# A new hand-written list of steps for the first three token blocks of a fused retention and snake-activation kernel

## The chip, the cores and the metric

The kernel runs on one core of one Trainium2 chip. The metric is device microseconds of one execution of the whole program on that core. The engines are named as in the profile: PE (TensorE, matmuls and transposes), DVE (VectorE), ACT (ScalarE), POOL (GpSimd), SP (SyncE, which here only issues DMAs).

## The reference, cut to what matters

Eight batches of 576 tokens with 8 heads of 64 go through a causal retention with a decay of its own for each head, and the result, with the heads side by side, is the input of a two-layer feed-forward net with a snake activation.

```python
scores = scale * q @ k^T                      # q, k, v: (8, 8, 576, 64) float32
ret    = scores * Dmat                        # Dmat[i, j] = gamma_h ** (i - j) for j <= i, else 0
attn   = ret @ v
x      = attn.transpose(0, 2, 1, 3).reshape(4608, 512)
h      = x @ w_in                             # 512 x 2048
g      = h + sin(alpha * h) ** 2 / (alpha + 1e-9)
out    = g @ w_out                            # 2048 x 512, float32
```

## The kernel before, in words

**Tiling.** The 4608 tokens are nine blocks of 512. Block n (0 to 7) holds the first 512 tokens of batch n; block 8 gathers the last 64 tokens of all batches. A batch's 512 tokens are two halves of 256, called p = 0 and p = 1; q, k and v of one batch and half are one tile of 512 KB in float32. Retention is done in chunks of 128: the scores of a chunk against itself (`scores`, then the mask by `masked` on DVE, L370), those times v (`values`, L400), and the state that the chunks before left (`outer`, L298, makes a chunk's sum of k and v; `take_sum` or `evict` copies it out of PSUM; `more`, L339 and L340, and `to_state`, L332, decay and add on POOL; `add_states`, L422, multiplies by q). `keep` copies the outcome into xT, a block's input.

**A block's feed-forward net.** The 2048 hidden features are 16 units of 128, called fc. `project(n, fc)` is four matmuls of 128x128 by 512 tokens against w_in (L535). Then come `sine` on ACT (L543), `square` on ACT, DVE or POOL (L552, L554) and `product` on DVE (L559), which writes gT. For blocks 0 and 1 `gemm2(n, u, tag)` does the second layer: u = 4c + part, c one of four groups of 128 tokens, part one of four quarters of w_out; each is four matmuls of 512 columns (L581). `finish(n, c)` copies a group out and stores it. From block 2 on the second layer is done by sums and products of halves (`Quarters`, L652), which needs sums of halves of w_out that `weigh(k, i)` makes (L602).

**Loads.** `load(b, nm, p)` issues one 512 KB tile on SP's queue (L121); six of these tiles have buffers (the tag "raw", bufs=6), so a load further on waits until a `cast` has read an older tile. `cast` brings a tile to half precision with the decay factors (L181 for q and k, L104 or L102 for v). The weights come in quarters by `load_w_in(g)` and `load_w_out(g)` on POOL's own DMA queue (L92, L95): 128x4x512 elements, float32 in DRAM and float16 in SBUF. For batches 0 and 1 q and k are transposed on PE (`turn`, L215) and copied out (`take`); from batch 2 on by DMA (`crossed`, L205, on SP).

**What sets the order.** The block `with tc.manual_schedule()` is a hand-written list of calls: every engine and every DMA queue runs its instructions in the order of that list, and an instruction that waits holds up all that stand behind it on its engine. Before the loop, the list covers retention of batches 0 to 4 and the nets of blocks 0, 1 and 2; the loop `for n in range(3, NBLK)` that follows does block n beside the retention of batch n + 1. `keep_busy` puts matmuls of zeros on PE; `told(x, engine)` puts a no-op on an engine that waits for instruction x.

In the list before, q(0,1) and k(0,1) are cast whole on POOL and DVE, w_in's quarters are issued in the order 0, 2, 1, 3, retention of batch 0 is done before the first `project`, block 0's units follow in the order 2, 1, 0, 8, 3, 11, 6, ... with two halves only where a piece is marked 0 or 1, batch 1's retention stands after the last of them among seven `gemm2` calls, and the other nine `gemm2` calls of block 0 stand among block 1's units.

## Time and profile before

| | us |
|---|---|
| median of 3 runs | 302.8 (300.9 to 302.86) |
| the profiled execution, its own time | 300.74 |
| its span | 299.0 |
| PE busy in the span | 284.0 (95%) |
| DVE, ACT, POOL busy | 224.0, 206.3, 196.7 |
| first `project` matmul on PE | 21.35 |
| first `project` of block 1 | 50.58 |
| first `project` of the loop (block 3) | 112.74 |

Times inside the program are microseconds from the start of the span. A row of the timeline gives the start, the length, the engine, the line, the operation with the tile written and the tiles read, the count, and in brackets the idle time of the engine just before it and what ended that wait. SPq, POOLq and ACTq are DMA issues. PEclk in the table of windows is the granted share of PE's full clock.

### The profile page before, as it was taken

The page shows a single profiled execution, that of the slowest core. Times are in us where ns is not written, and L with a number is a line of the kernel's source. Part 1 is how long each engine was busy: PE and PEld are TensorE (multiplying, and loading weights), DVE is VectorE, ACT ScalarE, POOL GpSimd, SP SyncE. Part 2 cuts the span into 40 slices and gives each one's busy share as a digit, 9 for nine tenths or more (in the row PEclk, how much of TensorE's full clock was granted, in tenths as well). Part 3 has the DMA queues.
Part 4 walks back from the last instruction along what each step waited for, and adds up shares of the span by engine and source line. Part 5 has one row for each costly group of instructions (what it writes and reads, how often), then busy time and mean ns, then how long its engine had stood idle before and what let it go on. Part 6 is the DMA issues. An engine that isn't in the chain of part 4 may idle for free.

```text
span 299.0 us, 8721 instructions
## 1 busy us (share of the span) xinstructions
PE 284.0 (95%) x3597; PEld 183.4 (61%) x3597; DVE 224.0 (75%) x316; ACT 206.3 (69%) x328; POOL 196.7 (66%) x186
## 2 busy tenths in 40 slices
PE   7689989999997999999999999999999999999993
PEld 6565545554442576665666666766666666665782
DVE  2597988789779897998779667876778476656871
ACT  1439944876546599776878787878777878887600
POOL 5794680899999789599897789769915900370000
PEclk9689999999999999999999999999999999999998
DMA  7999999999995397978699777587747201310225
GB/s 227 343 217 216 216 251 303 202 299 301 177 248 186 84 166 173 248 179 198 157 271 175 160 184 206 57 190 158 147 108 176 53 3 39 71 37 17 61 49 120
DMA packets 119159, 49.89 MB, mean 167 GB/s; under 512 B 69824, under 2 KB 118096, under 8 KB 119120
## 3 DMA queue, kind: packets, MB, share of 16 engines
q1 hardware_dynamic: 114528, 45.04, 65.8%
q0 software_dynamic: 4224, 4.19, 8.3%
q8 instruction: 28, 0.46, 0.7%
q10 hardware_dynamic: 368, 0.11, 0.2%
q14 instruction: 11, 0.09, 0.1%
HBM read 36.74 MB, written 9.44 MB: 154 GB/s over the span
## 4 chain that ended last, share of the span: by engine, by line
PE 59%; DMA 14%; POOL 11%; DVE 7%; issue 3%; ACT 2%; SPq 2%; POOLq 0%; DVEq 0%; ACTq 0%
PE hps L535 27%; PE hps L652 26%; DMA v<-in_v_dram 10%; DMA q<-in_q_dram 4%; POOL T L602 3%; POOL q L181 2%; DVE ret L370 2%; DVE gT L559 2%; POOL kvs L340 1%; ACT s_t L543 1%; PE o L400 1%; PE ops L581 1%; POOL s L339 1%; PE sc L358 1%; SPq L121 1%
## 5 line engine op out<-in xcount | busy, mean ns | idle before, releaser
L559 DVE SCALAR_TENSOR_TENSOR gT<-ss_t,inva,hps 128x512 f16<-128x512 f16 x144 | 105.6, 744 | 37.8 <-ACT ss_t L552 36.4
L543 ACT ACTIVATE s_t<-hps,alpha_t 128x512 f16<-128x512 f32 x144 | 96.7, 682 | 40.4 <-PE hps L535 39.7
L535 PE MATMUL hps<-xT,w_in 128*128 128x512 f16 (+1 forms) x564 | 121.2, 360 | 2.0 <-DVE gT L559 1.4
L535 PEld LDWEIGHTS <-w_in 128*128 128x128 f16 x628 | 60.1, 98 | 54.7 <-issue 3.3
L552 ACT ACTIVATE ss_t<-s_t 128x512 f16<-128x512 f16 x117 | 73.2, 630 | 3.2
L652 PEld LDWEIGHTS <-gT 128*128 128x128 f16 x656 | 63.9, 98 | 14.4
L624 POOL TENSOR_TENSOR gT<-gT,d 128x1024 f16<-128x1024 f16 x12 | 25.2, 2121 | 29.2 <-PE hps L652 28.1
L652 PE MATMUL hps<-T,gT 128*128 128x256 f16 x336 | 39.8, 273 | 0.0
L652 PE MATMUL hps<-w_out,gT 128*128 128x256 f16 x320 | 38.2, 273 | 0.0
L370 DVE TENSOR_TENSOR ret<-sc,mask 128x1024 f16<-128x1024 f32 (+1 forms) x32 | 34.8, 1117 | 3.8 <-PE sc L358 3.8
L672 DVE TENSOR_TENSOR osb<-osb,hps 128x512 f32<-128x512 f32 x35 | 24.0, 686 | 14.8 <-PE hps L652 13.7
L581 PE MATMUL ops<-w_out,gT 128*128 128x512 f16 x128 | 30.8, 379 | 2.1 <-DVE gT L559 1.4
L181 POOL TENSOR_TENSOR q<-q,cn 128x1024 f16<-128x1024 f32 (+1 forms) x16 | 27.8, 1747 | 4.1 <-DMA q<-in_q_dram 4.1
L630 POOL TENSOR_TENSOR gT<-gT 128x1024 f16<-128x1024 f16 x12 | 25.7, 2161 | 0.0
L181 POOL TENSOR_TENSOR k<-k,cn 128x1024 f16<-128x1024 f32 (+1 forms) x13 | 21.9, 1681 | 1.9 <-DMA k<-in_k_dram 1.9
L581 PEld LDWEIGHTS <-gT 128*128 128x128 f16 x128 | 11.9, 98 | 16.3 <-DVE gT L559 1.9
L340 POOL TENSOR_TENSOR kvs<-s,kvs 128x256 f32<-128x256 f32 x22 | 17.4, 789 | 3.7 <-ACT kvs L102 2.0
L332 POOL TENSOR_TENSOR s<-kvs,cn 128x256 f16<-128x256 f32 x21 | 14.2, 678 | 7.1 <-ACT kvs L102 6.5
L102 ACT COPY osb<-hps 128x512 f32<-128x512 f32 (+2 forms) x15 | 8.2, 549 | 13.5 <-PE hps L652 13.4
L102 ACT CAST xT<-o 128x1024 f16<-128x1024 f32 (+1 forms) x14 | 13.2, 956 | 5.6 <-PE o L422 5.6
L104 POOL CAST v<-v 128x1024 f16<-128x1024 f32 (+1 forms) x10 | 10.0, 1015 | 9.2 <-PE hps L535 6.7
L554 DVE TENSOR_TENSOR ss_t<-s_t 128x512 f16<-128x512 f16 x23 | 12.7, 554 | 3.2 <-ACT s_t L543 3.2
(77 smaller groups left out, 272.8 us busy)
## 6 DMA issues: line engine op xcount, KB each, us to landing
out_dram<-osb SPq DMA_DIRECT2D x70, 128.0 KB, 2.5
q<-in_q_dram SPq DMA_DIRECT2D x16, 512.0 KB, 5.7
k<-in_k_dram SPq DMA_DIRECT2D x10, 512.0 KB, 6.2
v<-in_v_dram SPq DMA_DIRECT2D x10, 512.0 KB, 5.8
k<-in_k_dram SPq DMA_DIRECT2D x24, 128.0 KB, 3.6
v<-in_v_dram SPq DMA_DIRECT2D x24, 128.0 KB, 3.4
w_in<-in_moe_w_in_dram POOLq DMA_DIRECT2D x4, 512.0 KB, 12.0
w_out<-in_moe_w_out_dram POOLq DMA_DIRECT2D x4, 512.0 KB, 11.5
```

Of the source, the lines that this page charges most:

```text
L102: eng.copy(d_, s_)
L181: eng.tensor_tensor(dst[:, a0:a1].rearrange("p a r t d -> p t (a r) d"), t_.rearrange("p (t a) x -> p t a x", t=2)[:, :, a0:a1].rearrange( ...
L370: nc.vector.tensor_tensor(ret.rearrange("p t (z x) -> p (t z) x", z=2)[:, :, 0:n], sc.rearrange("p t (z x) -> p (t z) x", z=2)[:, :, 0:n], ...
L535: matmul(hps_of[n, fc][0][:, cols], w_in16[:, a, fc * P : (fc + 1) * P], xs[n][:, a, cols], start=(a == 0 and part != 1), stop=(a == KT - ...
L543: nc.scalar.activation(s_t, hps, mybir.ActivationFunctionType.Sin, bias=0.0, scale=alpha_t[:, fc : fc + 1],)
L552: nc.scalar.activation(ss_t, s_t, mybir.ActivationFunctionType.Square)
L559: nc.vector.scalar_tensor_tensor(gT[n][:, :, fc, :], ss_t.rearrange("p (t n) -> p t n", t=2), inva[:, fc : fc + 1], hps.rearrange("p (t n) ...
L581: matmul(ops[n, c, cols.start][:, cols], gT[n][:, c // 2, fk, c % 2 * P : c % 2 * P + P], w_out16[:, fk, cols], start=(fk == 0), stop=(fk ...
L624: eng.tensor_tensor(self.part(0, 0, i), self.part(1, 1, i), self.d3[:, 4 * i : 4 * i + 4], SUB)
L630: eng.tensor_tensor(out_, self.part(1, 0, i), self.part(0, 0, i), SUB)
L652: matmul(self.ps[name][:, 256 * m + cols.start : 256 * m + cols.stop], left(j)[:, P * m : P * m + P], right(j)[:, cols], start=(tag is not ...
L672: nc.vector.tensor_tensor(out_, a, self.ps[ps], ADD)
```

## The change

The list of steps up to block 2 is written anew; the functions it calls stay as they are, but that `cast` now returns its instruction and the slots of batch 1's q tiles are swapped.

- Start: all six tiles of batch 0 are loaded first, each cast is done by halves of the heads, and every half is transposed, copied and used as it comes. `load_w_in(0)` and `load_w_in(1)` are put on POOL's queue behind a no-op that waits for the second half of q(0,0)'s cast; quarters 2 and 3 follow later, in the order in which the units need them.
- Block 0: the units go in order 0 to 15. Units 0 to 3 are begun with the first 256 tokens, before `values(1)` of batch 0. Six squares stand on POOL (2, 4, 6, 8, 10, 12) where there were four (3, 7, 12, 10), and between them the half casts of k(1,0) and q(1,0) and the quarters of w_out.
- Batch 1 is worked half by half after block 0's last unit, p = 0 first, among fourteen `gemm2` calls that fill three token groups side by side (banks h0, op and h2) and a fourth (h1); the last two `gemm2` calls of block 0 stand in block 1. `load_w_out(3)` stands behind batch 1's first `to_state`.
- `next_sum(3)` on DVE becomes `more(3)` on POOL, for batches 0 and 1. The two `weigh(1, ..)` now stand ahead of the two casts of batch 2's v.
- Block 1's units go in order 0 to 15; `gemm2(1, 0..2)` moves up into it. In block 2, square 11 and the cast of v(4,1) go from DVE to ACT, `weigh(4, 1)` from DVE to POOL. In the loop at n = 3, three of the six casts are put behind the two `s4` steps on POOL.

```diff
         load(0, "k", 0)
         load(0, "q", 0)
-        cast(0, "q", 0, V, (1,))
+        load(0, "v", 0)
+        load(0, "q", 1)
+        load(0, "k", 1)
+        load(0, "v", 1)
+        cast(0, "k", 0, V, (0,))
         cast(0, "k", 0, V, (1,))
-        cast(0, "k", 0, G_, (0,))
...
+        cast(0, "q", 0, V, (0,))
+        turned = cast(0, "q", 0, V, (1,))
+        told(turned, G_)
+        load_w_in(0)
+        load_w_in(1)
...
+        project(0, 0, "h0", 0)
+        project(0, 1, "h1", 0)
+        project(0, 2, "op", 0)
+        at[0].values(1, False, "m0")
         at[0].values(1, True)
         at[0].add_states(1)
+        at[0].keep(1, A_, V)
...
+        sine(0, 2)
+        square(0, 2, G_)
+        load_w_out(0)
...
+        square(0, 10, G_)
+        load_w_out(2)
+        turn(1, "k", 0, "m1")
+        project(0, 11, "h0")
...
+        at[1].outer((0,), "m0")
+        at[1].evict((0,), A_)
+        at[1].to_state(0, G_)
+        load_w_out(3)
+        at[1].more(1)
...
+        at[1].outer((1,), "m0")
+        at[1].evict((1,), A_)
+        at[1].more(2)
+        at[1].to_state(2, G_)
+        gemm2(0, 7, "h0")
...
+        at[1].more(3)
+        weigh(1, 0, G_)
         cast(2, "k", 1, V, (0,))
         load(3, "k", 1)
+        at[1].to_state(3, G_)
+        weigh(1, 1, G_)
+        cast(2, "v", 1, G_)
         cast(2, "v", 0, G_)
-        weigh(1, 0, G_)
-        weigh(1, 1, G_)
...
-        weigh(4, 1, V)
...
+        square(2, 11, A_)
+        cast(4, "v", 1, A_)
...
-        square(2, 11, V)
-        product(2, 11)
-        cast(4, "v", 1, V)
...
         at[3].to_state(0, G_)
+        weigh(4, 1, G_)
...
+            ahead = 3 if n == 3 else 6
             if n < 6:
-                for x in KEYS:
+                for x in KEYS[:ahead]:
                     cast(n + 2, *x, G_)
             Q.s4(0, G_)
             Q.s4(1, G_)
+            if n < 6:
+                for x in KEYS[ahead:]:
+                    cast(n + 2, *x, G_)
```

The orders below are those of the built programs. A name is a tile with its number: s_t and ss_t are the sine and its square, k32, q32 and v32 loaded tiles, k16, q16 and v16 cast ones, kvs and s32 the sums of a state, s16 and sS states, T1 what `weigh(1, ..)` makes. POOL while block 0's units run, before: the casts of batch 1 are whole ones, and few squares stand between them.

```order
L95 DMA w_out16_72<-in_moe_w_out_dram 128x4x512
L181 TENSOR_TENSOR q16_548<-q32_482,cn_66 128x2x8x64
L554 TENSOR_TENSOR ss_t_589<-s_t_579 128x512
L95 DMA w_out16_72<-in_moe_w_out_dram 128x4x512
L332 TENSOR_TENSOR sS_73<-kvs_229,cn_66 128x256
L95 DMA w_out16_72<-in_moe_w_out_dram 128x4x512
L554 TENSOR_TENSOR ss_t_636<-s_t_634 128x512
L181 TENSOR_TENSOR k16_684<-k32_682,cn_66 128x2x8x64
```

The same place on POOL now, from the square of unit 2 to that of unit 10:

```order
L554 TENSOR_TENSOR ss_t_554<-s_t_552 128x512
L95 DMA w_out16_72<-in_moe_w_out_dram 128x4x512
L554 TENSOR_TENSOR ss_t_575<-s_t_573 128x512
L181 TENSOR_TENSOR k16_586<-k32_294,cn_66 128x2x4x64
L554 TENSOR_TENSOR ss_t_596<-s_t_594 128x512
L95 DMA w_out16_72<-in_moe_w_out_dram 128x4x512
L554 TENSOR_TENSOR ss_t_618<-s_t_616 128x512
L181 TENSOR_TENSOR k16_586<-k32_294,cn_66 128x2x4x64
L554 TENSOR_TENSOR ss_t_639<-s_t_637 128x512
```

The second half of the cast of k(1,0) stands behind four squares, two issues of w_out and its own first half; on PE `turn(1, "k", 0)` waits for it ahead of unit 11.

POOL around the end of batch 1's states, before: the two casts of batch 2's v stand right behind the states, `weigh(1, ..)` follows, and then the casts of q(2,1) and q(3,1).

```order
L340 TENSOR_TENSOR kvs_835<-s32_1007,kvs_835 128x256
L104 CAST v16_1064<-v32_1062 128x1024
L104 CAST v16_1070<-v32_1060 128x1024
L602 TENSOR_TENSOR T1_1072<-w_out16_72 128x512 x2
L602 TENSOR_TENSOR T1_1075<-w_out16_72 128x512 x2
L181 TENSOR_TENSOR q16_1122<-q32_1120,cn_66 128x2x8x64
L181 TENSOR_TENSOR q16_1345<-q32_1124,cn_66 128x2x8x64
```

And now, from the sums that wait for `evict((1,))` on:

```order
L340 TENSOR_TENSOR kvs_827<-s32_1009,kvs_827 128x256
L332 TENSOR_TENSOR s16_829<-kvs_827,cn_66 128x256
L339 TENSOR_TENSOR s32_1088<-kvs_827,cn_66 128x256
L340 TENSOR_TENSOR kvs_827<-s32_1088,kvs_827 128x256
L602 TENSOR_TENSOR T1_1091<-w_out16_72 128x512 x2
L332 TENSOR_TENSOR sS_73<-kvs_827,cn_66 128x256
L602 TENSOR_TENSOR T1_1099<-w_out16_72 128x512 x2
L104 CAST v16_1102<-v32_889 128x1024
L104 CAST v16_1104<-v32_887 128x1024
L181 TENSOR_TENSOR q16_1141<-q32_1139,cn_66 128x2x8x64
L181 TENSOR_TENSOR q16_1352<-q32_1143,cn_66 128x2x8x64
```

`weigh(1, ..)`, one sum and two states moved ahead of the v casts; from the cast of q(2,1) on POOL's list is the same as before up to the last state of batch 3.

SP's queue behind batch 2's first five tiles, before: two transposes, then q(2,1) and q(3,1).

```order
L121 DMA k32_1068<-in_k_dram 128x8x128
L205 DMA_TRANSPOSE kT_1114<-k16_1112 128x8x128
L205 DMA_TRANSPOSE qT_1118<-q16_1116 128x8x128
L121 DMA q32_1120<-in_q_dram 128x8x128
L121 DMA q32_1124<-in_q_dram 128x8x128
```

And now:

```order
L574 DMA out_0_dram<-osb_1038 64x512 x2
L574 DMA out_0_dram<-osb_1079 64x512 x2
L574 DMA out_0_dram<-osb_1084 64x512 x2
L121 DMA k32_1096<-in_k_dram 128x8x128
L205 DMA_TRANSPOSE kT_1133<-k16_1131 128x8x128
L205 DMA_TRANSPOSE qT_1137<-q16_1135 128x8x128
L121 DMA q32_1139<-in_q_dram 128x8x128
L121 DMA q32_1143<-in_q_dram 128x8x128
```

Three stores of block 0's outcome moved ahead of the load of k(3,1), the transposes and the load of q(2,1).

More of the change, by code (lines that the diff above doesn't have):

```diff
@@ L864 @@
[L864 to L883 removed]
+        product(0, 0)
@@ L897 @@
+        square(0, 12, G_)
+        cast(1, "q", 0, G_, (0,))
+        project(0, 13, "op")
+        sine(0, 13)
+        square(0, 13, A_)
+        product(0, 12)
+        product(0, 13)
+        cast(1, "q", 0, G_, (1,))
+        take(1, "k", 0, A_, (0,))
+        take(1, "k", 0, V, (1,))
+        project(0, 14, "m0")
+        sine(0, 14)
+        square(0, 14, V)
+        project(0, 15, "h2")
+        product(0, 14)
+        turn(1, "q", 0, "m1")
         sine(0, 15)
         square(0, 15, A_)
+        gemm2(0, 4, "h0")
@@ L899 @@
+        gemm2(0, 12, "op")
+        take(1, "q", 0, V, (0,))
+        take(1, "q", 0, A_, (1,))
         product(0, 15)
[L900 to L913 removed]
```

457 lines of the change are left out of this document (213 added, 244 removed).

## The prediction, made before the run

> **What bounds the kernel now.** I read the profile's totals and its chain of waits first, then POOL's and PE's timelines, then a table of windows between the points that these gave. Totals, and the chain's shares by engine:
>
> ```profile
> PE 284.0 (95%) x3597; PEld 183.4 (61%) x3597; DVE 224.0 (75%) x316; ACT 206.3 (69%) x328; POOL 196.7 (66%) x186
> PE 59%; DMA 14%; POOL 11%; DVE 7%; issue 3%; ACT 2%; SPq 2%; POOLq 0%; DVEq 0%; ACTq 0%
> ```
>
> Over the whole span PE is the bound, but DMA and POOL hold a quarter of the chain, and all of the rewritten list lies in the first 104 us. POOL's timeline, and behind it the window from its cast of q(2,1) to its last state of batch 3 (span, then busy time of PE, PEld, DVE, ACT, POOL, then clock, DMA share, GB/s), and PE's rows for what follows, the second of them the loop's first `project`:
>
> ```profile
> 53.46 2.02 POOL L104 CAST v<-v 128x1024 f16<-128x1024 f32 x2 [6.74 <-PE hps L535]
> 55.44 4.49 POOL L602 TENSOR_TENSOR T<-w_out 128x512 f16<-128x512 f16 x4
> 60.54 3.76 POOL L181 TENSOR_TENSOR q<-q,cn 128x1024 f16<-128x1024 f32 x2 [0.61 <-DMA q<-in_q_dram]
> ...
> 101.25 0.61 POOL L332 TENSOR_TENSOR s<-kvs,cn 128x256 f16<-128x256 f32 x1
> ```
>
> ```profile
> 60.54:101.86 41.32, 39.37 (x482) 19.16 (x482) 36.26 (x44) 24.30 (x41) 40.61 (x41) 1.00 0.89 215
> ```
>
> ```profile
> 103.80 7.13 PE L535 MATMUL hps<-xT,w_in 128*128 128x512 f16 x52
> ...
> 112.74 1.89 PE L535 MATMUL hps<-xT,w_in 128*128 128x512 f16 x8
> ```
>
> The reader is to see that POOL is busy for 40.61 of 41.32 us without a break, and that 1.9 us after its last state PE has finished batch 3's retention and goes on at 103.80. So in blocks 1 and 2 two engines are full, PE and POOL, and the moment at which POOL can start this row of 41 instructions (60.54, set by a load of q) fixes how early it can end. From the order of the program the row holds the same instructions after the change. The question is when it starts.
>
> **The start.** The rows that price it are the landing of k(0,0), a half cast on DVE, the first issue of w_in with the time that its four quarters took to land, and PE's and ACT's last steps of batch 0:
>
> ```profile
> 4.83 1.04 POOL L181 TENSOR_TENSOR k<-k,cn 128x512 f16<-128x512 f32 x1 [0.74 <-DMA k<-in_k_dram]
> 6.29 0.69 DVE L181 TENSOR_TENSOR q<-q,cn 128x512 f16<-128x512 f32 x1 [5.06 <-DMA q<-in_q_dram]
> 11.18 1.68 POOL L92 DMA_DIRECT2D w_in<-in_moe_w_in_dram  x2
> ```
>
> ```profile
> DMA to landing us min/median/max: 8.9/12.0/12.8
> ```
>
> ```profile
> 19.85 1.08 PE L400 MATMUL o<-ret,v 64*64 64x128 f16 x32
> 20.76 0.40 PE L422 MATMUL o<-qT,s 64*64 64x128 f16 x16
> 21.35 2.06 PE L535 MATMUL hps<-xT,w_in 128*128 128x256 f16 x12 [0.19 <-DVE xT L104]
> ```
>
> DVE casts two halves of k from 4.8 to 6.2 and two of q from 6.3 to 7.7; POOL's no-op ends there and the first quarter is issued at 7.7, not 11.18. With the shortest landing, 8.9, it is there at 16.6, so `project` starts about 16.6 where it started at 21.35. But values of the second half (1.08 + 0.40) and a copy now stand behind three half units, where before they were done. Of 4.7 us some 1.7 go there: about 3.0 us of head start in PE's work, with ends of 1.5 (start at 18) and 4.7 (all of it).
>
> **POOL in block 0.** Means by shape of POOL's square, of its issue of w_out and of a half cast, of ACT's sine and square, and three units on PE:
>
> ```profile
> L554 POOL TENSOR_TENSOR ss_t<-s_t 128x512 f16<-128x512 f16 x4 | 4.1, 1036 | 6.7 <-ACT s_t L543 6.7
> L95 POOL DMA_DIRECT2D w_out<-in_moe_w_out_dram x4 | 3.2, 804 | 0.0
> L181 POOL TENSOR_TENSOR k<-k,cn 128x512 f16<-128x512 f32 x4 | 4.6, 1154 | 0.7 <-DMA k<-in_k_dram 0.7
> ```
>
> ```profile
> L543 ACT ACTIVATE s_t<-hps,alpha_t 128x512 f16<-128x512 f32 x144 | 96.7, 682 | 40.4 <-PE hps L535 39.7
> L552 ACT ACTIVATE ss_t<-s_t 128x512 f16<-128x512 f16 x117 | 73.2, 630 | 3.2
> ```
>
> ```profile
> 70.20 2.76 PE L535 MATMUL hps<-xT,w_in 128*128 128x512 f16 x12
> ```
>
> Three half units, the values and the copies take PE from 16.6 to about 21; three sines and a square on ACT (3 x 0.68 + 0.63 = 2.7) bring sine 2 to 23.8. From there POOL has no gap: four squares, two issues and two half casts, 4 x 1.04 + 2 x 0.80 + 2 x 1.15 = 8.1, so k(1,0) is whole at 31.9. PE stands before its transpose after unit 10: the second halves to about 22.8, then seven units of 0.86 (2.76 less the tail of the last, by 3), 6.0, and some 0.5 of waiting for banks, 29.3. It waits 2.6 us. The head start is gone at this place.
>
> **To the end of batch 1.** A transpose of a tile, a score, the values of both halves, a chunk's sum, a copy of it, and the landing of w_out:
>
> ```profile
> 17.59 0.62 PE L215 MATMUL tr<-ident,q 128*128 128x128 f16 x8
> 39.38 0.42 PE L358 MATMUL sc<-qT,kT 64*64 64x128 f16 x16
> 47.20 1.38 PE L400 MATMUL o<-ret,v 64*64 64x128 f16 x64
> 44.99 0.44 PE L298 MATMUL kv<-v,k 64*64 64x64 f16 x32 [0.66 <-ACT v L102]
> 45.48 0.37 ACT L102 COPY kvs<-kv 128x256 f32<-128x256 f32 x1 [0.55 <-PE kv L298]
> ```
>
> ```profile
> DMA to landing us min/median/max: 9.6/11.5/14.7
> ```
>
> From 31.9 to `outer((1,))` PE has five units (4.3), eleven `gemm2` calls of 0.86 (9.5) and the pieces of retention: four transposes (2.4), one sum and the values of one half (1.1), four scores of about 0.4. That is 18.9; in-order waits of PE on casts and copies of the same half (a turn waits for its cast, a score for its copy) add some 2: 52.8. The twelfth square on POOL and two half casts of q(1,0) fall under this. On the way `load_w_out(3)` is issued only after the first state of batch 1, about 46.2 by the same count, and lands at 55.8 at the earliest; `gemm2(0, 7)` wants it at 53.3, a PE wait of 2.5. I do not add it, since POOL's work runs on beside it; if POOL were not the bound, it would cost its 2.5.
>
> **POOL before its long row.** Means by shape of `weigh`, the sums and the states, and how long the load of q(2,1) took to land:
>
> ```profile
> L340 POOL TENSOR_TENSOR kvs<-s,kvs 128x256 f32<-128x256 f32 x22 | 17.4, 789 | 3.7 <-ACT kvs L102 2.0
> L339 POOL TENSOR_TENSOR s<-kvs,cn 128x256 f32<-128x256 f32 x22 | 14.2, 646 | 0.2
> L332 POOL TENSOR_TENSOR s<-kvs,cn 128x256 f16<-128x256 f32 x21 | 14.2, 678 | 7.1 <-ACT kvs L102 6.5
> L602 POOL TENSOR_TENSOR T<-w_out 128x512 f16<-128x512 f16 x8 | 9.6, 1229 | 0.0
> ```
>
> ```profile
> DMA to landing us min/median/max: 5.2/5.2/5.2
> ```
>
> `outer((1,))` and its copy of 512 columns (0.44 and twice 0.37 at most) end about 53.9. POOL then does 0.79 + 0.68 + 0.65 + 0.79, two halves of `weigh` (2.46), a state (0.65) and two more (2.46), 8.5 in all: the casts of v begin at 62.4, where they began at 53.46, and end at 64.4. Only these casts free the buffers that q(2,1) and its neighbour load into, and SP issues that load behind three stores and two transposes, which wait for casts on DVE: 64.7, landed 69.9. So POOL's long row starts at 69.9 instead of 60.54, 9.4 late. Of that, 5.6 come from `weigh`, sum and state being put ahead of the casts, the rest from PE's lateness in `outer((1,))`.
>
> **Sum.** 41.3 us later it ends at 111.2, and PE goes on 1.9 later, 113.1 instead of 103.80, +9.3. The row holds half casts at 1.15 beside 1.04 elsewhere, stretched by what ran beside them; with a us less of it I take +8.5. What is left, from 103.80 to 299.0, has the same instructions. 299.0 + 8.5 = 307.5 of span; the execution took 300.74, 1.7 more than its span: 309.2. The median of the runs is 2.1 above that execution and 302.8 + 8.5 is 311.3; between the two I say 310.
>
> **Edits that I price at nothing.** In block 2 DVE loses a square, a cast and a `weigh`. PE's table of waits has what that can bring:
>
> ```profile
> PE ops L581 <- DVE gT L559: 1.4, 1, 1.4
> PE hps L535 <- DVE gT L559: 1.4, 2, 0.7
> ```
>
> Up to 2.8 us, if POOL were not full there; under POOL's row it is covered, so 0, with ends of -2.8 and +0.5 (`weigh(4, 1)` costs POOL 2.46, but stands behind the row's last state, ahead of sums that waited for ACT before). In the loop at n = 3 two `s4` move ahead of three casts: both feed steps a third of a block later, 0 with ends of -0.5 and +1. `more(3)` instead of `next_sum(3)` is in POOL's sum above; the swapped slots of q and the other order of block 1's units move no duration. Half casts and half copies at the start lie ahead of 16.6, beside the landing of w_in.
>
> **Clock.** One transpose tile at half clock, beside 0.62 above, and the window in which the clock was down:
>
> ```profile
> 11.29 1.04 PE L215 MATMUL tr<-ident,q 128*128 128x128 f16 x8 [0.97 <-POOL q L181]
> ```
>
> ```profile
> 10.00:15.00 5.00, 4.03 (x58) 2.97 (x56) 3.59 (x6) 2.60 (x5) 4.91 (x6) 0.53 1.16 339
> ```
>
> If it falls again, a piece costs 0.4 more and the two or three on the path about 1 us; if it does not, nothing. I take 0, since the landing of w_in at 16.6 covers most. The Trainium skill (TensorE: Matmul & The Clock Gate, Part 4) says that PE transposes do not count as activity for the gate; by that the new start, with more of them spread out, would run at half clock and the sum be 311.
>
> **Rivals.** (a) DMA at the start. SP's issue of one tile is held to the pace at which tiles move, without and with w_in in flight:
>
> ```profile
> 6.28 1.45 SPq L121 DMA_DIRECT2D v<-in_v_dram  x1
> ```
>
> ```profile
> 20.96 7.01 SPq L121 DMA_DIRECT2D v<-in_v_dram  x1
> ```
>
> A tile takes 1.45 alone and 7.01 beside w_in. If the sooner quarters begin to move while v(0,1) is half loaded, its rest takes 3.5 instead of 0.7, and `outer((1,))` of batch 0 with all behind it, `project` too, starts up to 3 us later: 310 + 1.5 = 311.5. The Trainium skill (DMA: Bandwidth & Descriptors, "Issuing engines are not separate DMA queues") says just that, that queues share the same engines and interleave; the two rows agree. Chance 0.10.
>
> (b) PE short of other work in block 1. Nine `gemm2` calls of block 0 (7.8 us of PE) stood among its units to fill waits for DVE's products; two do now. DVE was busy 36.26 of the 41.32 us above. If DVE stretches the row by half of the seven missing calls, 3 to 4 us: 314. Chance 0.18.
>
> (c) About the same. POOL's row starts by 63 because PE comes through batch 1 with fewer waits than the 2.6 and 2 that I count and SP's transposes do not hold the load: 302.8 + 2 = 305. Chance 0.10.
>
> (d) Faster. POOL's lateness is absorbed: if its cast of q(2,1) begins by 57.5, the 3.0 of head start pass through to the end, and the relief of DVE in block 2 adds one of its waits, 1.4: 302.8 - 4.4 = 298.4. For it speaks that `project` surely starts sooner; against it, that 8.1 us of POOL stand between sine 2 and a transpose on which PE waits in order, and `weigh` ahead of the casts. It decides at 60.5: before that there is a gain, after it a loss. Chance 0.07.
>
> **Numbers.** The forecast, POOL's late row, has the remaining 0.55. The range takes in (a), most of (b) and the upper half of (c): 304 to 314.5. One per cent, 3 us, is about what a measurement can tell from no change: faster by more 0.06, within it 0.11 (nearly all of (c), and a little of (d)), slower 0.83.
>
> **What would show it.** Right: first `project` near 16.6 and w_in issued near 7.7; PE idle about 2.6 before a transpose of k, ended by POOL's cast; `load_w_out(3)` issued near 46 and a PE wait for it; POOL's cast of q(2,1) near 70 with some 41 us without a break behind it; first `project` of the loop near 121 where it was 112.74 + 8.5. Wrong: POOL's row starting before 63, or starting near 70 but PE going on before 108; then POOL is not what sets blocks 1 and 2.

## The result, and the profile after

The changed kernel takes 313.27 us (median of 4 runs, 311.91 to 316.35), the kernel before on the same chip 302.36 us (300.9 to 302.86). The ratio is 1.0387, with a 95% interval of 1.0329 to 1.0445: 11 to 12 us slower. The profiled execution took 313.39 us, its span 311.7.

Totals of the changed kernel, and its chain of waits by engine:

```profile
PE 288.3 (93%) x3570; PEld 182.7 (59%) x3570; DVE 227.0 (73%) x308; ACT 207.7 (67%) x333; POOL 203.8 (65%) x199
PE 63%; POOL 19%; issue 5%; DVE 4%; DMA 3%; ACT 3%; SPq 1%; POOLq 0%; DVEq 0%; ACTq 0%
```

POOL's share of the chain went from 11% to 19%, that of DMA from 14% to 3%: by this chain the first transfers no longer hold the kernel, and POOL holds it for longer. POOL's timeline, in the rows that answer to those of the prediction (start, duration, line, operation, and in brackets how long POOL had been idle, and until what):

```profile
48.80 0.61 POOL L332 TENSOR_TENSOR s<-kvs,cn 128x256 f16<-128x256 f32 x1 [7.26 <-ACT kvs L102]
49.36 0.80 POOL L95 DMA_DIRECT2D w_out<-in_moe_w_out_dram  x1
...
59.65 2.78 POOL L602 TENSOR_TENSOR T<-w_out 128x512 f16<-128x512 f16 x2
62.39 1.05 POOL L332 TENSOR_TENSOR sS<-kvs,cn 128x256 f16<-128x256 f32 x1
63.41 4.22 POOL L602 TENSOR_TENSOR T<-w_out 128x512 f16<-128x512 f16 x2
67.58 2.21 POOL L104 CAST v<-v 128x1024 f16<-128x1024 f32 x2
72.80 3.76 POOL L181 TENSOR_TENSOR q<-q,cn 128x1024 f16<-128x1024 f32 x2 [3.01 <-DMA q<-in_q_dram]
...
112.76 0.61 POOL L332 TENSOR_TENSOR s<-kvs,cn 128x256 f16<-128x256 f32 x1
```

The long row starts at 72.80, 12.3 us later than before, and takes 40.6. The second pair of `weigh` pieces took 4.22 where the first took 2.78 and where four took 4.49 before. PE's timeline at the first `project`, at the transposes of k(1,0), in block 1, at the end of POOL's row and at the loop's first `project`:

```profile
17.92 2.09 PE L535 MATMUL hps<-xT,w_in 128*128 128x256 f16 x12
...
33.29 0.61 PE L215 MATMUL tr<-ident,k 128*128 128x128 f16 x4 [2.12 <-POOL k L181]
...
55.66 0.45 PE L298 MATMUL kv<-v,k 64*64 64x64 f16 x32
...
68.82 1.04 PE L535 MATMUL hps<-xT,w_in 128*128 128x512 f16 x4 [2.34 <-DVE gT L559]
...
111.85 0.31 PE L422 MATMUL o<-qT,s 64*64 64x128 f16 x8 [0.26 <-POOL s L332]
...
113.42 0.31 PE L422 MATMUL o<-qT,s 64*64 64x128 f16 x8 [1.04 <-POOL s L332]
...
124.01 1.89 PE L535 MATMUL hps<-xT,w_in 128*128 128x512 f16 x8 [1.37 <-DVE gT L559]
```

The start is 3.4 us earlier than before (17.92, was 21.35), the loop 11.3 later (124.01, was 112.74). PE's waits for POOL at the end of the row are small, 0.26 and 1.04: PE itself was hardly earlier there than POOL. That was not in the prediction, and it is what most of the experiments are about. In the kernel before there was no such wait at all. PE's timeline of the kernel before, in block 2 and where it uses the row's last state:

```profile
90.95 2.15 PE L535 MATMUL hps<-xT,w_in 128*128 128x512 f16 x8 [0.32 <-DVE ret L370]
...
96.26 3.63 PE L581 MATMUL ops<-w_out,gT 128*128 128x512 f16 x16 [1.43 <-DVE gT L559]
...
103.58 0.29 PE L422 MATMUL o<-qT,s 64*64 64x128 f16 x8
```

POOL was done with its last state at 101.86 and PE came to use it at 103.58, 1.7 us later, without waiting. What PE did wait for here was DVE.

To see where PE falls behind, whatever the order of its work, I add up PE's matmuls from the start in both traces, every kind counted with the mean interval between its starts in the kernel before and the idle matmuls left out, and read at equal sums how much later the other kernel is. For the profiled execution of the changed kernel, at the times of before in the first row (us):

```
before       26.5  32.5  46.7  59.2  65.8  85.0  99.6 106.1 115.6 138.6 229.7
changed      -0.9  +3.2  +3.7  +6.2  +8.4 +10.5  +8.2  +9.9 +11.3 +12.4 +12.6
```

So 4.1 us go at the transposes of k(1,0), 2.5 in batch 1's retention, 2.2 at the wait for DVE at 68.8, 2.1 in the rest of block 1. Then 2.3 come back where the kernel before stood still, mostly for DVE in the rows just shown, and 1.7, 1.4 and 1.1 go at the end of POOL's row, at the loop's first `project` and in block 3. Behind that nothing changes.

### The profile page after: what moved, and what is told of

Read it like the earlier page. It is cut to its first block, busy times and chain, and to the rows that moved or that the text cites. A ratio compares the mean times of both kernels' runs of the same rounds, so it can differ in the third digit from the quotient of the medians.

```text
span 311.7 us, 8684 instructions
## 1 busy us (share of the span) xinstructions
PE 288.3 (93%) x3570; PEld 182.7 (59%) x3570; DVE 227.0 (73%) x308; ACT 207.7 (67%) x333; POOL 203.8 (65%) x199
## 4 chain that ended last, share of the span: by engine, by line
PE 63%; POOL 19%; issue 5%; DVE 4%; DMA 3%; ACT 3%; SPq 1%; POOLq 0%; DVEq 0%; ACTq 0%
PE hps L535 27%; PE hps L652 26%; POOL T L602 5%; POOL q L181 3%; POOL kvs L340 2%; PE ops L581 2%; DMA k<-in_k_dram 2%; PE sc L358 2%; POOL s L332 2%; DVE gT L559 2%; POOL k L181 2%; POOL s L339 2%; PE o L400 1%; PE tr L215 1%; PE kv L298 1%
## 5 line engine op out<-in xcount | busy, mean ns | idle before, releaser
L535 PE MATMUL hps<-xT,w_in 128*128 128x512 f16 (+1 forms) x564 | 123.4, 364 | 6.0 <-DVE gT L559 4.8
L652 PEld LDWEIGHTS <-gT 128*128 128x128 f16 x656 | 63.8, 98 | 14.9 <-issue 0.6
L581 PE MATMUL ops<-w_out,gT 128*128 128x512 f16 x128 | 31.7, 380 | 0.5 <-DVE gT L559 0.3
L181 POOL TENSOR_TENSOR q<-q,cn 128x1024 f16<-128x1024 f32 (+1 forms) x17 | 25.9, 1541 | 3.1 <-DMA q<-in_q_dram 3.0
L332 POOL TENSOR_TENSOR s<-kvs,cn 128x256 f16<-128x256 f32 x24 | 15.3, 641 | 15.0 <-ACT kvs L102 14.2
L340 POOL TENSOR_TENSOR kvs<-s,kvs 128x256 f32<-128x256 f32 x24 | 19.1, 794 | 7.1 <-ACT kvs L102 5.3
L581 PEld LDWEIGHTS <-gT 128*128 128x128 f16 x128 | 11.5, 98 | 13.9 <-DVE gT L559 1.8
L102 ACT CAST xT<-o 128x1024 f16<-128x1024 f32 (+1 forms) x15 | 13.9, 931 | 7.9 <-PE o L422 7.9
L181 POOL TENSOR_TENSOR k<-k,cn 128x1024 f16<-128x1024 f32 (+1 forms) x12 | 18.5, 1540 | 0.0
L102 ACT COPY kvs<-kv 128x512 f32<-128x512 f32 (+2 forms) x15 | 8.3, 561 | 13.9 <-PE kv L298 10.8
L554 DVE TENSOR_TENSOR ss_t<-s_t 128x512 f16<-128x512 f16 x21 | 14.6, 695 | 3.9 <-ACT s_t L543 3.9
```

What stands on the lines that cost most here:

```text
L102: eng.copy(d_, s_)
L181: return eng.tensor_tensor(dst[:, a0:a1].rearrange("p a r t d -> p t (a r) d"), t_.rearrange("p (t a) x -> p t a x", t=2)[:, :, a0:a1].rea ...
L340: nc.gpsimd.tensor_tensor(self.kvs[:, c], s32, self.kvs[:, c], ADD)
L535: matmul(hps_of[n, fc][0][:, cols], w_in16[:, a, fc * P : (fc + 1) * P], xs[n][:, a, cols], start=(a == 0 and part != 1), stop=(a == KT - ...
L581: matmul(ops[n, c, cols.start][:, cols], gT[n][:, c // 2, fk, c % 2 * P : c % 2 * P + P], w_out16[:, fk, cols], start=(fk == 0), stop=(fk ...
L652: matmul(self.ps[name][:, 256 * m + cols.start : 256 * m + cols.stop], left(j)[:, P * m : P * m + P], right(j)[:, cols], start=(tag is not ...
```

## Experiments

Ratios are to the kernel before on the same chip, with their 95% intervals; 0.01 is 3.0 us. By these intervals e8, e11 and e13 differ from the changed kernel by more than the noise; e1, e6, e7, e9 and e12 do not, and what is said of their gains rests on the rows of their traces. "Lag" is the figure just described.

**e1, v cast first.** POOL's order alone is put back as it was before:

```
+ cast(2, "v", 1, G_); cast(2, "v", 0, G_)
  at[1].more(3) ... at[1].to_state(3, G_)
+ weigh(1, 0, G_); weigh(1, 1, G_)        (both stood ahead of the casts of v)
```

> The changed kernel with one move on POOL: the two casts of v(2,1) and v(2,0) stand ahead of batch 1's last sum, its last state and both weigh(1, .), as they did before. As the prediction has it (POOL's order costs 5.6 us of the late row): the casts begin near 59.7 instead of 67.58, the load of q(2,1) follows at once, POOL's cast of q(2,1) begins near 68 instead of 72.80, and the time falls by 4 to 5 us, to about 309. Refined theory: the load waits for two things that end within a microsecond of each other, POOL's cast of v (68.7) and SP's transpose of q(2,0) ahead of it in its queue (67.9, behind a cast on DVE); with the first gone the second stays, the load is issued near 67.5, the row starts near 72 and the time falls by 0.5 to 1.5 us. Rival (PE short of other work, DVE stretched): within 0.5 us of the changed kernel.

Ratio 1.0365 (1.0282 to 1.0449), not to be told from the changed kernel. POOL's timeline of e1:

```profile
55.53 2.02 POOL L104 CAST v<-v 128x1024 f16<-128x1024 f32 x2
...
59.91 7.08 POOL L602 TENSOR_TENSOR T<-w_out 128x512 f16<-128x512 f16 x4
70.61 3.76 POOL L181 TENSOR_TENSOR q<-q,cn 128x1024 f16<-128x1024 f32 x2 [3.62 <-DMA q<-in_q_dram]
```

The casts came 12 us sooner, the long row 2.2 sooner, and this execution had been 2.7 ahead already at batch 1's first state (46.07, not 48.80): the order on POOL gains the row nothing. The load of q still stood behind SP's transposes, which wait for casts on DVE. The 5.6 us that the prediction laid to POOL's order are not there. The refined theory, that the second wait stays, held in the row; its gain of 0.5 to 1.5 us can't be told here from the rival's nothing.

**e7, also the load sooner.** e1, and `load(2, "q", 1)` moved ahead of `crossed(2, 0, "k")` and `crossed(2, 0, "q")`.

> e1_v_casts_first and one move on SP: the load of q(2,1) stands ahead of the two DMA transposes of batch 2's first half. Refined theory: both waits gone, the load is issued near 63.5 and lands near 68, POOL's cast of q(2,1) begins near 69 (POOL then still has weigh and a state ahead of it) and the time falls by 3 to 4.5 us against the changed kernel, to about 309 to 310. Prediction as it stands: no more than e1 gives. Rival (filler): within 1 us of the changed kernel.

Ratio 1.0368 (1.0269 to 1.0468). POOL cast q(2,1) at 68.16, but the next tile only at 71.74, since the load of q(3,1) stands behind the same transposes. At the end of the row PE's timeline of e7 shows no wait for POOL, and then this:

```profile
111.73 0.29 PE L422 MATMUL o<-qT,s 64*64 64x128 f16 x8
111.95 0.61 PE L535 MATMUL hps<-xT,w_in 128*128 128x512 f16 x2
114.32 6.68 PE L535 MATMUL hps<-xT,w_in 128*128 128x512 f16 x50 [1.76 <-issue]
```

With the waits for POOL gone PE stood 1.76 us in the next unit, where it waits for nothing that the profile shows. The theory's 3 to 4.5 us did not come.

**e6, weigh in POOL's idle time.** e7, and

```
  at[0].to_state(3, G_)
+ weigh(1, 0, G_); weigh(1, 1, G_)        (moved here from behind at[1].to_state(3))
```

> e7_v_casts_and_load with both weigh(1, .) moved into POOL's idle time of 7.3 us between batch 0's last state and batch 1's first (from 41.5). Theory: POOL's cast of q(2,1) waits only for the landing of its load, near 67 to 68, so that the row begins about 5 us sooner than in the changed kernel and ends 5 us sooner: 308 to 309. Every microsecond by which the row starts sooner should be a microsecond of the time, to within 1. Rival (PE short of gemm2 units in block 1, DVE stretched): POOL's row gets longer by what it starts sooner, and the time falls by under 1.5.

Ratio 1.0324 (1.0238 to 1.0411), some 1.9 us better than the changed kernel, which is within the noise. The profiled execution was the slowest of its four (313.69, the others 309.85 to 311.12), so single rows are compared here and not its end. DVE's casts for batch 2 and its next square in the changed kernel, and then in e6:

```profile
60.74 3.79 DVE L181 TENSOR_TENSOR k<-k,cn 128x512 f16<-128x512 f32 x3
64.45 2.17 DVE L181 TENSOR_TENSOR q<-q,cn 128x1024 f16<-128x1024 f32 x1
66.54 1.37 DVE L554 TENSOR_TENSOR ss_t<-s_t 128x512 f16<-128x512 f16 x1
```

```profile
62.70 3.40 DVE L181 TENSOR_TENSOR k<-k,cn 128x512 f16<-128x512 f32 x3
66.02 1.21 DVE L181 TENSOR_TENSOR q<-q,cn 128x1024 f16<-128x1024 f32 x1
67.15 0.41 DVE L554 TENSOR_TENSOR ss_t<-s_t 128x512 f16<-128x512 f16 x1
```

Without `weigh` beside them the cast of q takes 1.21, not 2.17, and the square 0.41, not 1.37. PE's wait of 2.34 at 68.82 is gone, with the same two `gemm2` calls as filler; the lag falls by 2.3 there. So that wait was DVE slowed beside POOL, not a lack of filler. Expected was 4 to 5 us; the row's second cast began only 1.5 sooner, net of what e6 was late earlier.

**e2, weigh first in the kernel before.** The reverse of e1 on the other kernel: `weigh(1, 0, G_)` and `weigh(1, 1, G_)` ahead of the two casts of v.

> The kernel before with one move on POOL: both weigh(1, .) stand ahead of the casts of v(2,1) and v(2,0), all else as it was. Theory (the start of POOL's long row sets the time): the casts of v begin near 58 instead of 53.46, the load of q(2,1) is issued near 59 to 60, POOL's cast of q(2,1) begins at 64.5 to 66 instead of 60.54, and the time is 4 to 5.5 us longer than before, about 307. If POOL starts weigh sooner, since it had been idle for 6.7 us ahead of the casts, the loss is smaller by what it starts sooner; then the row's start and the time still move by the same amount. Rival (filler and DVE): no change, within 1 us.

Ratio 1.0067 (1.0025 to 1.0109): 2.0 us slower, half of what the theory gave or less. POOL, DVE and PE in e2:

```profile
46.25 5.57 POOL L602 TENSOR_TENSOR T<-w_out 128x512 f16<-128x512 f16 x4
```

```profile
48.37 2.43 DVE L181 TENSOR_TENSOR k<-k,cn 128x512 f16<-128x512 f32 x2
50.73 1.37 DVE L332 TENSOR_TENSOR sS<-kvs,cn 128x256 f16<-128x256 f32 x1
```

```profile
56.20 1.52 PE L535 MATMUL hps<-xT,w_in 128*128 128x512 f16 x4 [2.17 <-DVE osb L104]
```

In the kernel before the same casts of k took 1.29 and the state 0.42. The lag of e2 is 3.8 already where before stood at 56.2 and e2 at 59.9, ahead of POOL's row (63.02, 2.5 late), and 2.1 at the end. So the loss came by DVE, as in the changed kernel, and nearly half of it was absorbed behind. Part of the 3.8 is the clock, which stood at 0.50 from 56.59 to 60.00. The run does not refute the prediction's theory: the row began 2.5 later and the time is 2.0 longer, which is what the expectation says for a smaller delay. PE shows no wait for POOL at the end of the row here either.

**e4, block 2 and the loop alone**, on the kernel before: `square(2, 11)` and `cast(4, "v", 1)` from DVE to ACT, `weigh(4, 1)` from DVE to POOL, `ahead = 3 if n == 3 else 6`.

> The kernel before with the change's edits in block 2 (a square, a cast and a weigh off DVE) and in the loop at n = 3 alone. Prediction: priced at nothing, within -2.8 to +1.5 us of before; theory: within 1 us, so that the whole loss lies in the list up to block 1. Rival: the 1.3 us lost in block 3 comes from the loop's edit, then about 1 us slower.

Ratio 1.0002 (0.9964 to 1.0040): nothing, as predicted, and no loss in block 3 either. By themselves these edits cost nothing; what they do beside the new list no run shows. The profiled execution shows one thing more. By chance its clock was low for longer at the start, so that its first `project` came at 24.91, 3.6 us late; the lag of 4.5 fell to 3.0 at 47, 0.8 at 100 and 0.4 at the end. The first 1.5 went in a list that e4 shares with the kernel before; e2, e14 and e15, whose start was 1.0 to 1.2 late, lost 1.4 to 1.5 there too. The 2.3 between 85 and 100 went where PE of the kernel before waits for DVE, which e4 has relieved; e2, which has not, lost 1.6 there.

**e9, the transposes of k(1,0) later.** In the changed kernel `turn(1, "k", 0, "m1")` moves from behind `project(0, 10)` to behind `project(0, 12)`.

> The changed kernel with PE's transposes of k(1,0) behind project(0,12) instead of project(0,10); their copies stand where they stood. Theory (PE's own lateness in block 0 is carried on to everything behind it): the wait of 2.1 for POOL's half cast of k goes, PE, outer((1,)), the row on POOL and the end come 1.5 to 2.1 sooner, to about 311. Theory as predicted (POOL's row alone): the same, since outer((1,)) feeds POOL; the two agree here. Rival (block 1's lack of filler or DVE sets the time): under 0.5 us, since what PE gains it waits for later.

Ratio 1.0342 (1.0305 to 1.0380), 1.4 us better, within the noise. PE no longer waits there and is 3.7 us ahead of the changed kernel at 32.5 in the table's time; of that 1.9 is left at the end. The wait for DVE in block 1 stands, 2.41 (2.34 in the changed kernel), and behind it the clock was at half from 66.47 to 69.88, which it was not in the changed kernel. Reaching batch 1 sooner, PE now waited for the last quarter of w_out:

```profile
53.19 1.02 PE L581 MATMUL ops<-w_out,gT 128*128 128x512 f16 x4 [1.00 <-DMA w_out<-in_moe_w_out_dram]
```

**e8, no weigh in the row.** Six `weigh` calls leave the place ahead of POOL's row and the row itself:

```
  at[0].to_state(3, G_)
+ weigh(1, 0, G_); weigh(1, 1, G_); weigh(3, 0, G_)
  at[1].to_state(1, G_)
+ weigh(2, 0, G_)
  at[1].to_state(3, G_)
+ weigh(3, 1, G_); weigh(2, 1, G_)
  (v cast first; load(2, "q", 1) and load(3, "q", 1) ahead of crossed(2, 0, .))
```

> The changed kernel with all six weigh calls that stood before or in POOL's long row moved into POOL's idle times of block 0 and batch 1 (three after batch 0's last state, one after batch 1's second state, two after its last), with v cast first and with the loads of q(2,1) and q(3,1) ahead of batch 2's transposes on SP. The row then has 9 to 10 us less in it and starts no later than in e6. Theory as predicted (POOL's row alone sets the time): it ends 9 to 12 us sooner and nearly all of that comes back, to about 302 to 304. Refined theory (PE is itself about 8 us late by 72 us from its own waits in block 0 and batch 1, and POOL's row adds only what it is later than that): the waits of PE and ACT for POOL's last states go (1.0 to 1.3 and 2.9 in the changed kernel) and the DVE wait of 2.3 at 68.8 goes, so 4 to 6 us come back, to about 307 to 309, and PE, no longer POOL, is the chain from 70 to 112. Rival (filler alone): no better than e6_weigh_in_idle_time, 310.5.

Ratio 1.0294 (1.0234 to 1.0353), 2.8 us better, where the prediction's theory gave 9 to 12. POOL and PE in e8:

```profile
67.54 3.76 POOL L181 TENSOR_TENSOR q<-q,cn 128x1024 f16<-128x1024 f32 x2
...
89.50 0.61 POOL L339 TENSOR_TENSOR s<-kvs,cn 128x256 f32<-128x256 f32 x1 [5.29 <-ACT kvs L102]
```

```profile
108.39 0.61 PE L535 MATMUL hps<-xT,w_in 128*128 128x512 f16 x2
110.56 6.68 PE L535 MATMUL hps<-xT,w_in 128*128 128x512 f16 x50 [1.56 <-issue]
```

POOL starts 5 us sooner, has 9 us less to do and idles 5.29 us in what was the row; PE never waits for it at the end. Still the lag is 6.9 at 85, and a stop of 1.56 us with nothing awaited, as in e7, stands in the place of the waits for POOL. This is the run on which the prediction's theory falls: POOL's row was not what alone held PE. The refined theory asked for 4 to 6 us, which the interval reaches and the median does not.

**e11, e8 and e9 together.**

> e8_no_weigh_in_row and e9_transpose_later together. Theory (two separate losses, one on PE in block 0 and one on POOL in blocks 1 and 2): the gains add, 1.5 to 2 us below e8_no_weigh_in_row, about 305 to 307. If POOL's row alone set the time, e11 would be no better than e8 once the row is out of the way, or both would already be at the time of the kernel before.

Ratio 1.0497 (1.0418 to 1.0575): 6 us worse than e8. POOL, DVE and PE in e11:

```profile
37.05 4.47 POOL L602 TENSOR_TENSOR T<-w_out 128x512 f16<-128x512 f16 x4
```

```profile
36.22 5.58 DVE L554 TENSOR_TENSOR ss_t<-s_t 128x512 f16<-128x512 f16 x1
```

```profile
42.97 0.64 PE L358 MATMUL sc<-qT,kT 64*64 64x128 f16 x16 [4.28 <-DVE qT L104]
```

DVE's square, 0.41 us alone, ended only when POOL's four pieces of `weigh` had ended. In e8 the same square began 1.0 us ahead of those pieces and was through in 0.60; in e11 it began 0.8 ahead of them, while POOL was still in a cast (to 36.52) and had a state (to 37.09) between. The gains do not add when a move brings two such instructions together.

**e12, without that collision.** As e11, but `weigh(3, 0)` first in the idle time (it waits for its quarter of w_out), then `weigh(1, 0)`; `weigh(1, 1)` in batch 1; `weigh(2, 1)` behind batch 3's last state. `weigh(3, 1)` and `weigh(2, 0)` stay in POOL's row, as in the changed kernel.

> e11_both mended: the transposes of k(1,0) stand later as in e9, v cast first and both loads of q sooner as in e8, but POOL's idle time in block 0 begins with weigh(3,0), which has to wait for the third quarter of w_out (about 41.5), so that DVE's square at 36 is done before POOL's stream of f16 work begins; weigh(1,0) follows, weigh(1,1) stands in batch 1's idle time, weigh(2,1) behind batch 3's last state, and none stands beside DVE's casts of batch 2. Theory (three separate losses: PE's wait in block 0, DVE's casts stretched beside weigh with the PE wait of 2.3 behind them, POOL's row): DVE's square at 36 takes 0.4 to 1.2 instead of 5.6, no PE wait over 1 us stands between 62 and 75, and the time is 5 to 6.5 us below the changed kernel's, a ratio of 1.018 to 1.023 to before, 306 to 307.5. Rival (the change's block 1 lacks gemm2 calls to fill waits, whatever POOL does): PE still waits 2 us for DVE near 66 and the ratio stays at 1.029 or above.

Ratio 1.0357 (1.0307 to 1.0408). The theory's number failed. POOL and PE in e12:

```profile
42.47 6.08 POOL L602 TENSOR_TENSOR T<-w_out 128x512 f16<-128x512 f16 x4 [4.97 <-DMA w_out<-in_moe_w_out_dram]
```

```profile
49.18 0.31 PE L422 MATMUL o<-qT,s 64*64 64x128 f16 x8 [3.41 <-POOL s L332]
...
67.28 1.04 PE L535 MATMUL hps<-xT,w_in 128*128 128x512 f16 x4 [0.19 <-DVE gT L559]
```

The quarter came at 42.5, the four pieces ran beside DVE's casts and took 6.08, and batch 1's first state was late: my own move made a new wait of 3.41. What it does settle is block 1: PE's wait for DVE there is 0.19.

**e13, the remedies without either collision.** e9; both `weigh(1, .)` behind `at[1].to_state(1)`; v cast first and both loads sooner; `weigh(2, 1)` behind batch 3's last state.

> The changed kernel with the remedies that worked alone and without the two collisions of e11 and e12: the transposes of k(1,0) behind project(0,12), no weigh in block 0's idle time, both weigh(1, .) in the 4 us that POOL idles between batch 1's two halves, v cast first, the loads of q(2,1) and q(3,1) ahead of the transposes on SP, weigh(2,1) behind batch 3's last state. Theory (the loss is a sum of PE's wait in block 0, 1.4 to 2.1, DVE's casts of batch 2 stretched beside weigh with a PE wait of 2.3 behind them, and 1 to 2.5 at the end of POOL's row): 4.5 to 6.5 us below the changed kernel, a ratio of 1.017 to 1.024 to before; what is left, some 6 us, is PE's own path through batch 1 and blocks 2 and 3. As predicted (POOL's row alone sets blocks 1 and 2): its start moves by about 6 to 8 us, hence 6 to 8 us, a ratio of 1.012 to 1.018. Rival (block 1 lacks gemm2 calls as filler): the ratio stays above 1.029.

Ratio 1.0279 (1.0232 to 1.0326), 3.2 us better than the changed kernel, below the 4.5 that the theory asked for; the interval reaches both that and the rival's 1.029. PE in e13, and its chain of waits:

```profile
53.48 1.02 PE L581 MATMUL ops<-w_out,gT 128*128 128x512 f16 x4 [1.12 <-DMA w_out<-in_moe_w_out_dram]
...
70.61 0.42 PE L358 MATMUL sc<-qT,kT 64*64 64x128 f16 x16 [1.84 <-DMA qT<-q]
...
110.21 6.68 PE L535 MATMUL hps<-xT,w_in 128*128 128x512 f16 x50 [1.55 <-issue]
```

```profile
PE 72%; DVE 9%; DMA 6%; POOL 4%; issue 4%; ACT 2%; SPq 1%; DVEq 0%; POOLq 0%; ACTq 0%
```

The waits at k(1,0), for DVE in block 1 and for POOL's row are gone, and others of 1 to 2 us took their places, all on transfers or on nothing that is shown. POOL's share of the chain is 4%. The lag: -0.3 at 32.5, 0.0 at 46.7, +3.4 at 59.2, +5.0 at 65.8, +6.6 at 85, +6.0 at 106 and 7.9 at the end.

**e14 and e15, the kernel before with a shorter row.** e14: `weigh(2, 1)` behind batch 3's last state, `weigh(4, 1)` from DVE to POOL behind batch 4's. e15: also the change's other edits of block 2 and the loop.

> The kernel before with POOL's long row shortened by one weigh: weigh(2,1) moved behind batch 3's last state, and weigh(4,1) moved from DVE to POOL behind batch 4's last state. Theory (in the kernel before POOL's row does set the time of blocks 1 and 2, and PE waits some 2.4 us for it between 88 and 104): PE goes on at 101.5 to 102 instead of 103.80 and the time is 1.5 to 2.4 us below before's, a ratio of 0.992 to 0.995. Rival (PE's own work and waits set it, the row's end is only near by): within 0.7 us of before. Against both: weigh(4,1) delays POOL's s2 in block 3, then up to 1 us slower.

> e14_before_shorter_row with the change's other edits of block 2 (a square and a cast from DVE to ACT) and its edit in the loop. Theory: they were worth nothing beside a full POOL (e4), but with the row shortened PE's waits for DVE's products are the next limit, so 0 to 1 us below e14. Rival: the same as e14 within 0.5 us.

e14: ratio 0.9963 (0.9916 to 1.0011), not clear of no change; e15: ratio 0.9947 (0.9902 to 0.9992), clear of it by little. PE's row behind batch 3's retention in e14, where before had 103.80:

```profile
101.78 7.13 PE L535 MATMUL hps<-xT,w_in 128*128 128x512 f16 x52
```

PE goes on 2.0 sooner, as the theory said, but the rows give another reason. DVE's cast of k in block 2, in the kernel before and in e14, and the last state of POOL's row in e14:

```profile
91.95 2.29 DVE L181 TENSOR_TENSOR k<-k,cn 128x512 f16<-128x512 f32 x1
```

```profile
91.00 1.23 DVE L181 TENSOR_TENSOR k<-k,cn 128x512 f16<-128x512 f32 x1
```

```profile
98.06 0.61 POOL L332 TENSOR_TENSOR s<-kvs,cn 128x256 f16<-128x256 f32 x1
```

e14 also takes `weigh(4, 1)` off DVE, where the kernel before spent 1.09 us on it after a wait of 0.35 for POOL; DVE's cast starts 0.95 sooner and takes 1.06 less, and PE's waits of 0.32 and 1.43 for DVE are gone. The last state of POOL's row is done at 98.67 and PE uses it at 101.56, without a wait, as in the kernel before. So the end of POOL's row is not what PE waits for in either; the 2 us came by DVE. Which of e14's two moves brought them no run separates. In the traces the lag is -2.2 (e14) and -3.1 (e15) at the end; the ratios give 1.1 and 1.6 us, so that e15 is half a per cent faster than the kernel before.

## Why the prediction was right, and where its reason was not

The time was 313.3 against 310.0 predicted, inside 304.0 to 314.5, and slower as said. Step by step:

- **The start.** Right to half a microsecond at its first event: w_in was issued at 8.02 (7.7) and its first quarter landed at 16.61 (16.6). The first `project` began at 17.92, not 16.6: the half units waited for retention work of PE ahead of them, at half clock from 15.8 to 19.2. The head start, by the lag at 26.5, was 0.9 in this execution and 2.0 to 2.4 in seven of the eight experiments with the same start (3.0, with ends of 1.5 and 4.7); in e6 PE was 0.8 late there.
- **POOL in block 0.** Right: PE waited 2.12 (2.6) before the second half of k(1,0), ended by POOL's cast. The wait alone was not the price: 4.1 us of lag arose there. The clock fell to half from 32.89 to 36.30. e9 takes the wait away and gets 1.4 back, within the noise.
- **To the end of batch 1.** `outer((1,))` came at 55.66 (52.8), `load_w_out(3)` was issued at 49.36 (46.2). PE did not wait 2.5 for it, being later itself; when it was sooner, in e9 and e13, 1.0 and 1.1 of this wait came out.
- **POOL before its long row.** Right in kind, and larger: 72.80 (69.9). But "Of that, 5.6 come from `weigh`, sum and state being put ahead of the casts" is wrong: e1 undoes this order and the row starts no sooner, since SP's transposes hold the load as well. I had named both waits and priced one. What `weigh` ahead of the casts did do is stretch DVE's casts beside it, which I had not priced (e6, e2).
- **The sum.** PE went on at 113.66 (113.1), so the working seemed to hold to 0.6 us. The step that failed is the one on which it rests, that the start of POOL's row fixes when PE goes on: "The question is when it starts." The prediction took the 1.9 us between the row's last state and 103.80 for a tie between the two engines; PE's rows of the kernel before, above, show no wait for POOL there, and 1.7 us to spare. In the changed kernel the last state was 11.5 later (112.76, was 101.25), and less the 1.7 that gives 9.8 for PE. But by then PE was 8 us late on its own account, by a wait in block 0, batch 1's pieces and a wait for DVE, and POOL was late by about as much. e8 took 9 us of work off POOL's row and 2.8 us came back, not 9. Two limits had come to lie close together, and I took the one for the cause. That the sum came within 0.6 us of this event is luck in so far as PE's lateness, which the sum does not hold, nearly equalled POOL's.
- **What lay behind it.** The term +8.5 measured +9.9 at the end of the row and +12.6 at the end of the span. ACT's copy of batch 4's sums, the first row below, had to wait for POOL's last state of batch 3, since one buffer holds the sums, and PE then waited 1.37 for DVE; this wait is not there in e8 and e13. The rest, between the loop's first `project` and the end of block 3, is 0.7 to 1.9 in every version of the changed list and not in e4, so it is not the loop's edit alone. What it is stays open. A second buffer for the sums was not tried.

ACT's timeline of the changed kernel at that place:

```profile
113.40 0.58 ACT L102 COPY kvs<-kv 128x512 f32<-128x512 f32 x1 [2.90 <-POOL s L332]
```

- **Edits priced at nothing.** Right as a sum: e4, 1.0002, to within 1.2 us. The reason given, that POOL's row covers PE's waits for DVE, is not what the rows show: these waits stand in PE's rows of the kernel before, and no wait for POOL does. In e4 they are gone.
- **The clock.** Priced at 0, up to +1, and too low: behind the wait in block 0 alone the stretch at half clock is worth up to 1.7, as worked out in the last section.
- **The rivals.** (a) did not arise: the second half of v(0,1) was there when POOL came to cast it, at 14.9, without a wait. (b) gave 314, nearest to the result, and its DVE wait was there, but not for its reason: with the same two `gemm2` calls it went from 2.34 to 0.19 in e12 once `weigh` stood elsewhere. (c) and (d) needed the row to start by 63 and by 57.5; it started at 72.80.

Of the loss of some 11.5 us, e13 gives back 3.2. What is left in it arises mainly between 47 and 66 of the table's time (5.0 of lag). Of that, 3.4 come while batch 1's retention is worked half by half among the `gemm2` calls and block 1 begins, with waits of 0.4 to 1.1; the rest is the wait of 1.84 for a transposed tile. No run took that arrangement back, so that its share is argued from the trace, not shown. Why the sooner start did not pay is in part a question to the kernel before: a start that was 1 to 4.5 us late lost 1.4 to 1.5 of its lateness by 47 (e2, e4, e14, e15). By that a start 3 us sooner could have lost as much again to what else is waited for there, even if nothing else had moved; this is an inference, no run had the new start with the old blocks.

## What to carry to other kernels

When one engine's unbroken row ends just as another needs it, look first whether the second waits for it at all, and then ask how late the second would be without it: compare the two at equal work, not at the end of the row alone. Price a moved instruction also by what runs beside it at its new place, above all an f16 stream on POOL against DVE. A wait of PE of 2 us or more is to be priced with what the clock may add, and a remedy that works alone is measured again with the others.

## What the runs showed of the hardware

**A wait of PE can cost twice.** In these executions the granted clock falls to half for a stretch of about 3.4 us around the end of many waits of PE of 2.1 us and more. The changed kernel at the wait of 2.12, e9 behind its wait of 2.4 for DVE and e12 behind its wait of 3.41 (stretch, busy time of PE, PEld, DVE, ACT, POOL, then the clock):

```profile
32.89:36.30 3.41, 3.01 (x11) 1.36 (x12) 0.90 (x2) 0.66 (x1) 2.09 (x3) 0.50 1.19 293
```

```profile
66.40:69.80 3.40, 3.40 (x10) 1.21 (x8) 2.75 (x5) 2.38 (x4) 0.25 (x1) 0.51 0.92 261
```

```profile
49.65:53.05 3.40, 3.40 (x15) 1.48 (x13) 0.00 (x0) 2.46 (x4) 3.22 (x5) 0.51 1.07 187
```

Half of 3.4 us, 1.7, is lost where PE has no slack; this is an estimate from the two numbers. It does not follow every such wait. Between 22 and 125 us the traces hold 13 waits of 2.1 us and more, and nine of them have such a stretch, e11's 4.28 one of twice the length (42.28 to 49.10). Four have none: 2.34 in the changed kernel, 2.12 in e1 and in e8, 2.11 in e11. No stretch begins there without such a wait. e13's execution, whose longest wait is 1.84, shows none up to 300 us, although it has the same start. The Trainium skill (TensorE: Matmul & The Clock Gate, Part 1) speaks of a free-running window of about 3.4 us; the length agrees here, and a window that does not start with the wait would explain why a wait of 2 us meets it in some executions only. Its rule on transposes, which the prediction weighed, does not settle this start: e13 ran the same spread transposes, with idle matmuls between them, at the full clock.

**POOL and DVE hold each other up, and DVE can starve.** A square of 128x512 in f16 took 0.41 us on DVE alone, 1.37 beside `weigh`, and 5.58 in e11, where a cast, a state and four pieces of `weigh` followed each other on POOL without a gap. The Trainium skill (SBUF — State Buffer, "SBUF: two separate sides") says that one port pair is held by one of the two for a whole instruction; the trace fits this for one instruction, and shows more: here the loser was kept out over six in a row.

**Time that no wait explains.** In e7, e8, e11, e12 and e13 PE stands 0.98 to 1.76 us in block 2's first unit behind batch 3's retention with nothing awaited, always behind the same two matmuls. In e1 and e9, which wait 0.60 for POOL just ahead of it, 0.42 and 0.35 are left, and in the changed kernel and e6, which wait 1.04 there, nothing; the kernel before and its variants do not have it. The traces hold one thing that goes with it. On the queue that the page calls instruction, a transfer of 16 KB starts 2.3 to 3.0 us ahead of the end of the gap in each of these seven versions (in e8 it runs from 107.6 to 109.0, and PE goes on at 110.56); in the kernel before it starts at 104.6, when PE had gone on at 103.80. That PE waited for its own instructions is a guess from this, and no run tested it. If it holds, the small waits for POOL at the end of the row cost next to nothing, since this gap takes their place.
